# A row DFT moved one pass later, rows normalised four tiles ahead, and nine row tiles transposed by DMA

## The chip, the cores and the metric

The kernel runs on one core of a Trainium2 chip. The metric is the device time of one execution in microseconds (us). A core has a matrix engine (TensorE, PE), a vector engine (VectorE, DVE), an engine for activation functions (ScalarE, ACT), a general one (GpSimd, POOL) and one that does little but issue transfers (SyncE, SP). Each works through its own queue of instructions in order and waits on semaphores for the others; DMA transfers are issued by SP, ACT or POOL and run beside all engines.

## What is computed

The input x has 2048 rows of 576. Its rows are normalised, and two branches work on the result: branch A is a filter in the frequency domain (2D FFT over rows and columns, product with complex weights, inverse), branch B a gated MLP whose gate mixes the 2048 rows with a 2048x2048 matrix.

```python
def _A_ref(x, w_r, w_i):
    X = rfft2(x.astype(float32), axes=(-2, -1))
    X = X * (w_r + 1j * w_i)
    return irfft2(X, s=(S, D), axes=(-2, -1)).astype(bfloat16)

def _B_ref(x, w_in, w_sp, b_sp, w_out):
    z = gelu(einsum('bsd,df->bsf', x, w_in))          # w_in 576 x 4608
    z1 = z[..., :Fh]                                  # Fh = 2304
    z2 = layernorm(z[..., Fh:], axis=-1)
    g = einsum('ts,bsf->btf', w_sp, z2) + b_sp[None, :, None]
    return einsum('bsf,fd->bsd', z1 * g, w_out)

xn = layernorm(A_x, axis=-1)
return A_x + _A_ref(xn, ...) * silu(_B_ref(xn, ...))
```

## The kernel before

**Row tiles and passes.** The 2048 rows are 16 tiles of 128 (m = 0 to 15). For each tile DVE computes mean and variance in `ln1` (L282: two `bn_stats` of 288 columns, L270, and one `bn_aggr`, L274). `rstd_of` (L259) has POOL make the factor 1/sqrt(var + eps) in two small instructions: `ve` (L261) and a power, `pow` (L263). `ln1_apply` (L289) writes the normalised row on DVE into XN, of which there are three buffers (L293, L296). `xpose` (L300) transposes it on TensorE in five blocks of 128x128 (L304), and ACT copies the result from PSUM into xnT (L305). xnT feeds both branches.

**Branch A.** The FFT is a chain of matrix products. `p0_fold` (L309) forms sums and differences of the two halves of a row tile on DVE (L311, L312); FS has four buffers for them. `p0` (L325, with `p0_tail`, L316) is the DFT along the row, on TensorE into PSUM, of which branch A has two buffers. `p0_out` (L332) copies it out on ACT (L334), and **POOL issues the DMA to the scratch Ad in DRAM (L336)**. When all 16 tiles are written, `p1_read` (L342, on SP) reads Ad back the other way round and `p1` (L344) does the first half of the column DFT; p2 (with the weights), p3, p4 and p5 follow, each with a way through DRAM or SBUF between.

**Branch B.** z = gelu(xn @ w_in) comes in chunks. A z2 chunk (L449) is 128 rows by 384 columns; there are 96, six for each row tile. A z1 chunk (L544) is 128 columns by 512 rows; there are 72, and they go to DRAM. Each chunk has four matmuls of 128 rows of contraction and a fifth of 64 (the tail); tails of two chunks at a time are put side by side in the array. z2 rows are normalised like x: for most tiles by six DVE `bn_stats` of chunks (L485), an aggregate (L501), `rstd_of` on POOL and one wide DVE operation (L503). For five tiles ACT makes the sums instead. After the last chunk the mixing with w_sp runs as `main` (L607): a Strassen scheme with seven products P1 to P7 for each of 27 units. It needs sums of z2 blocks (`tsum`, L593, three of a unit) and of slabs of w_sp (`slab_sums`, L536, in parts 0, 1 and 2), both on DVE for the first unit. `outm` (L662) multiplies by w_out and ends the work.

**Order.** Within `tc.manual_schedule` (L740) the instructions of SP, PE and DVE run in the order in which the code issues them; ACT's and POOL's order is chosen by the framework. The chunks fill the time in which branch A waits: `fill(n)` (L709) issues the next n chunks on TensorE in the order of the string `kinds` (L697, "2" for z2, "1" for z1). DVE's work on z2 is queued in `stats_q` and `norm_q`, and `spend` and `z2_stats` (L512, L517) let it out by a running estimate of DVE's and TensorE's load; with `fill(1, 0)` as in the pass loop, hardly any is let out.

**The head and the loop.** The first loads are issued at L247 to L256. From L757 the head normalises tiles 0 to 4 and does passes 0 and 1; the loop of L773 does pass m = 2 to 15. One pass on DVE is fold(m), statistics of tile m+3, apply(m+2); on TensorE it is p0 of the tile, two transposes in every other pass, and two chunks. After the loop come four p1 reads and `fill(11)`.

```python
p0_fold(m)
if m + 3 < MT:
    ln1(m + 3)
if m + 2 < MT:
    ln1_apply(m + 2)
```

Of the kernel before, what the change touches and what calls it, by code (L numbers as in the profile page):

```python
# [90 lines left out]
def kernel(  # L91
# [137 lines left out]

    def load_win_main(t, fs, eng=nc.sync):  # L230
        for a in range(2):
            eng.dma_start(out=t[:, a:KS - 1:2, :], in_=wv[a, 0:2 * P, fs].rearrange("(b p) f -> p b f", p=P))
# [14 lines left out]
    nc.scalar.dma_start(out=ident[:], in_=cd_id.ap())  # L247
    for m0, m1 in ((0, 1), (1, 2), (2, 4)):
        nc.sync.dma_start(out=XC[0][:, m0:m1, :], in_=xv[:, m0:m1, :])
    for n in range(2):  # L250
        load_win_main(WIN2[:, :, n * ZC:(n + 1) * ZC], slice(Fh + n * ZC, Fh + (n + 1) * ZC), nc.scalar)
    for g in range(3):
        (load_win if g else load_win_tail)(WIN2[:, :, 2 * g * ZC:2 * (g + 1) * ZC], slice(Fh + 2 * g * ZC, Fh + 2 * (g + 1) * ZC))
        if g == 0:
            nc.sync.dma_start(out=CDSD, in_=cd_cdsd.ap().rearrange("p (a k l) -> p a k l", a=2, k=3))
        load_x(g + 1)  # L256
    nc.sync.dma_start(out=G1, in_=cd_g1.ap().rearrange("p (s k) -> p s k", s=N2))

    def rstd_of(mv, n, tag):  # L259
        ve = small.tile([P, n], F32, tag=tag + "v")  # L260
        nc.gpsimd.tensor_scalar(out=ve[:], in0=mv[:, :, 1], scalar1=1e-5, scalar2=one[:, 0:1], op0=ALU.add, op1=ALU.mult)  # L261
        rs = small.tile([P, n], F32, tag=tag + "r", bufs=5)
        nc.gpsimd.tensor_tensor(out=rs[:], in0=ve[:], in1=mhalf[:, 0:n], op=ALU.pow)  # L263
        return rs
# [7 lines left out]
    def ln1_aggr(m):  # L272
        mv = small.tile([P, 1, 2], F32, tag="mv1", bufs=5, name="mv1")
        nc.vector.bn_aggr(out=mv[:, 0, :], in_=st1[m][:])  # L274
        if m == 0:
            rs = small.tile([P, 1], F32, tag="l11r", bufs=5, name="rs1")
            nc.scalar.activation(out=rs[:], in_=mv[:, :, 1], func=ACT.Sqrt, bias=eps[:], scale=1.0)
        else:
            rs = rstd_of(mv, 1, "l11")
        ln1_of[m] = (mv[:, 0, 0:1], rs[:, 0:1])  # L280

    def ln1(m):  # L282
        ln1_stats(m)
        ln1_aggr(m)

    st1 = {}
    ln1_of = {}
# [11 lines left out]

    def xpose(m):  # L300
        xn = XN[m % 3]
        pt = psh.tile([P, KS, P], BF16, tag="h")
        for ks in range(KS):
            nc.tensor.transpose(pt[:, ks, :], xn[:, ks * P:(ks + 1) * P], ident[:])  # L304
        nc.scalar.activation(out=xnT[:, m, :, :], in_=pt[:], func=ACT.Identity)  # L305

# [389 lines left out]
    tick = [0]  # L696
    kinds = "2" * 32 + "221" * 11 + "21" * 20 + "221" * 9 + "2111" * 4  # L697
    kinds += "2" * (MT * NZC - kinds.count("2")) + "1" * (FT * 4 - kinds.count("1"))
# [41 lines left out]
    with tc.manual_schedule(engines={SP, PE, DVE}):  # L740
# [19 lines left out]
        ln1_apply(0)  # L760
        nc.scalar.activation(out=THF[:, 0:1], in_=ln1_of[0][1], func=ACT.Gelu_apprx_tanh)
        xpose(0)
        ln1_stats(1, (1,))
        ln1_aggr(1)
        keep_warm(2)
        fill(1, 0)
        ln1(2)
        ln1_apply(1)
        p0_fold(0)
        ln1_apply(2)  # L770
        ln1(3)
        fill(1, 0, lambda: p0_pair(0), lambda: (xpose(1), p0(0, True), xpose(2)))
        p0_fold(1)  # L773
        ln1_apply(3)
        p0(1, False)
        p0_out(1)
        ln1(4)
        fill(1, 0)
        fill(1, 0)
        nc.sync.dma_start(out=MM, in_=cd_mm.ap().rearrange("p (a k) -> p a k", a=3))  # L780
        for m in range(2, MT):
            if m % 2 == 0:
                xpose(m + 1)
            spend(0.78, 2.35 if m + 3 < MT else 0.6)
            p0_fold(m)
            if m + 3 < MT:
                ln1(m + 3)
            if m + 2 < MT:
                ln1_apply(m + 2)
            if m % 2 == 0:  # L790
                fill(1, 0)
                fill(1, 0, lambda: p0_pair(m), lambda: p0(m, True))
            else:
                p0(m, False)
                p0_out(m)
                fill(1, 0)
                if m + 1 < MT:
                    xpose(m + 1)
                fill(1, 0)
            if m in (6, 9):  # L800
                load_win1(m // 9)
        for ch in range(4):
# [17 lines left out]
        for hh in range(0, N2, 2):  # L820
            fill(2)
            if hh + 2 < N2:
                p2(hh + 2)
                spend(0.25, 1.5)
            if hh % 8 != 6:
                fill(1)
            p3(hh)
            spend(0.5)
# [28 lines left out]
        z2_stats(99)  # L857
        for w in (0, 2, 1):
            tsum(0, w)
        later.append(partial(slab_sums, 2, 0, 2))  # L860
# [5 lines left out]
        fill(len(kinds) - place[0])  # L866
        z1_store(None, None)
        assert not stats_q and not norm_q
        for i in range(2):
# [50 lines left out]
```

## Time and profile before

| | |
|---|---|
| median of three runs | 500.8 us (500.46 to 501.24) |
| the profiled execution | 500.46 us, of which the span of the profile is 498.7 us |
| TensorE's clock granted over the span | 1.00 |
| instructions on TensorE | 3454 matmuls in the records (45 row-tile transposes of the change's tiles 7 to 15 among them) |

The slices of the page (40 of 12.5 us each, busy share in tenths) show how the work of the engines lies over the span:

```profile
PE   7999999999999999899999999999999999999996
DVE  5776588798656797965665648856666547877634
ACT  4878777686878656200000011100000011000001
POOL 2665223434242684445535400455454311666600
DMA  7961678978372998672111599021111863111202
```

The first slice holds the loads and the first row tiles, the slices two to four the passes; branch A and the chunks last to about 203 us, and the mixing with w_sp and the product with w_out fill the rest. The costliest groups (columns: line, engine, operation, operands, count, then busy us and mean ns of one, then idle time before and what ended it) that bear on the change:

```profile
L458 PE MATMUL ph<-AR 128*128 128x384 bf16 (+1 forms) x480 | 89.6, 327 | 1.1 <-DMA AR<-in_B_w_in_dram 0.6
L554 PE MATMUL ph<-AR 128*128 128x512 bf16 (+1 forms) x360 | 85.9, 379 | 0.0
L617 PE MATMUL pm<-AR 128*128 128x384 bf16 (+1 forms) x648 | 107.0, 308 | 2.0 <-DVE AR L540 1.9
```

And the transfers that are issued on POOL and read back by SP (columns: KB of one, us from issue to landing):

```profile
Ad<-AR POOLq DMA_DIRECT2D x16, 144.5 KB, 3.6
AR<-Ad SPq DMA_DIRECT2D x4, 578.0 KB, 6.0
```

### The profile page before, as it was taken

The numbers are of one execution on the slowest core, as the hardware profiler recorded it, in microseconds if no ns is written. First come the engines' busy times: TensorE is split into PE (matmuls) and PEld (weight loads), VectorE is DVE, ScalarE is ACT, GpSimd is POOL, SyncE is SP. The second block draws the span as 40 slices with busy tenths as digits, with TensorE's granted clock in tenths as the row PEclk, the third lists the DMA queues.
The fourth block names the chain that finished last, engine by engine and source line by source line (L and its number), as shares of the span: only waits on it lengthen the run. The fifth ranks groups of instructions, "written<-read, shape, count | busy, mean of one in ns | idle before, by whom it ended". The sixth has DMA issues, their size and how long they took to land.

```text
span 498.7 us, 9373 instructions
## 1 busy us (share of the span) xinstructions
PE 488.7 (98%) x3454; PEld 309.5 (62%) x3454; DVE 341.5 (68%) x747; ACT 169.6 (34%) x355; POOL 207.5 (42%) x280
## 2 busy tenths in 40 slices
PE   7999999999999999899999999999999999999996
PEld 3666454555556544466666678666666678888885
DVE  5776588798656797965665648856666547877634
ACT  4878777686878656200000011100000011000001
POOL 2665223434242684445535400455454311666600
PEclk9999999999999999999999999999999999999999
DMA  7961678978372998672111599021111863111202
GB/s 234 312 212 49 251 265 262 315 228 240 109 257 73 242 270 234 202 235 64 33 46 50 125 166 219 27 61 34 48 48 33 174 135 99 50 46 47 76 27 70
DMA packets 86766, 70.67 MB, mean 142 GB/s; under 512 B 39776, under 2 KB 79328, under 8 KB 86464
## 3 DMA queue, kind: packets, MB, share of 16 engines
q1 hardware_dynamic: 80480, 55.54, 41.9%
q0 software_dynamic: 5008, 13.71, 8.2%
q10 hardware_dynamic: 1232, 0.82, 0.5%
q8 instruction: 27, 0.44, 0.4%
q14 instruction: 19, 0.16, 0.1%
HBM read 40.40 MB, written 21.26 MB: 124 GB/s over the span
## 4 chain that ended last, share of the span: by engine, by line
PE 89%; ACT 4%; DVE 3%; DMA 2%; issue 1%; SPq 0%; DVEq 0%; ACTq 0%
PE pm L617 43%; PE po L671 13%; PE ph L554 13%; PE ph L458 12%; PE pb L386 2%; PE pa L329 1%; DMA AR<-in_A_x_dram 1%; PE pa L428 1%; PE pa L374 1%; ACT AR L334 1%; ACT Z_74 L471 1%; PE pa L350 1%; ACT Z_74 L477 1%; PE pa L402 1%; DMA AR<-c_cdsd 1%
## 5 line engine op out<-in xcount | busy, mean ns | idle before, releaser
L617 PE MATMUL pm<-AR,Z_74 128*128 128x384 bf16 (+1 forms) x864 | 138.7, 308 | 0.0
L621 DVE TENSOR_TENSOR AR<-pm,AR 128x384 f32<-128x384 f32 (+3 forms) x162 | 82.4, 513 | 70.2 <-PE pm L617 66.5
L617 PEld LDWEIGHTS <-Z_74 128*128 128x128 bf16 x864 | 84.5, 98 | 40.6
L617 PE MATMUL pm<-AR 128*128 128x384 bf16 (+1 forms) x648 | 107.0, 308 | 2.0 <-DVE AR L540 1.9
L458 PE MATMUL ph<-AR 128*128 128x384 bf16 (+1 forms) x480 | 89.6, 327 | 1.1 <-DMA AR<-in_B_w_in_dram 0.6
L554 PE MATMUL ph<-AR 128*128 128x512 bf16 (+1 forms) x360 | 85.9, 379 | 0.0
L617 PEld LDWEIGHTS <-AR 128*128 128x128 bf16 x648 | 63.3, 98 | 32.8 <-DVE AR L540 2.2
L631 ACT ACTIVATE AR<-pm 128x384 f32<-128x384 f32 (+1 forms) x27 | 12.3, 455 | 187.4 <-PE pm L617 187.4
L671 PE MATMUL po<-AR 128*128 128x288 bf16 x540 | 66.6, 286 | 0.0
L671 PEld LDWEIGHTS <-AR 128*128 128x128 bf16 x594 | 56.9, 98 | 13.9
L458 PEld LDWEIGHTS <-AR 128*128 128x128 bf16 (+1 forms) x480 | 40.0, 97 | 36.8 <-issue 14.5
L605 POOL TENSOR_TENSOR AR<-Z_74,AR 128x1024 bf16<-128x1024 bf16 x26 | 55.3, 2128 | 12.1 <-PE pm L617 12.1
L632 POOL TENSOR_TENSOR AR<-AR 128x384 f32<-128x384 f32 (+1 forms) x27 | 22.9, 849 | 79.7 <-ACT AR L631 75.6
L574 POOL DMA_DIRECT2D Z1d<-AR x55 | 32.0, 582 | 55.7 <-ACT AR L563 53.2
L554 PEld LDWEIGHTS <-AR 128*128 128x128 bf16 (+1 forms) x360 | 30.2, 97 | 28.1 <-issue 5.5
L563 ACT ACTIVATE AR<-ph 128x512 bf16<-128x512 f32 x72 | 42.1, 593 | 15.6 <-PE ph L554 15.4
L477 ACT ACTIVATE Z_74<-ph 128x384 bf16<-128x384 f32 x66 | 31.9, 500 | 23.4 <-PE ph L458 23.2
L674 ACT ACTIVATE TH<-po 128x576 f32<-128x576 f32 x15 | 9.8, 651 | 77.8 <-PE po L671 77.8
L635 POOL TENSOR_TENSOR AR<-AR 128x384 f32<-128x384 f32 (+1 forms) x27 | 30.1, 1114 | 12.5 <-DVE AR L621 12.5
L628 DVE TENSOR_TENSOR AR<-AR 128x384 bf16<-128x384 bf16 (+1 forms) x108 | 31.7, 334 | 0.9
L680 DVE SCALAR_TENSOR_TENSOR AR<-TH,po 128x576 bf16<-128x576 f32 x15 | 11.3, 754 | 30.0 <-ACT TH L674 29.9
L686 POOL DMA_DIRECT2D out_dram<-AR x12 | 6.6, 548 | 52.4 <-DVE AR L684 46.0
(186 smaller groups left out, 504.0 us busy)
## 6 DMA issues: line engine op xcount, KB each, us to landing
Z1d<-AR POOLq DMA_DIRECT2D x55, 128.0 KB, 4.2
AR<-Z1d SPq DMA_DIRECT2D x36, 192.0 KB, 3.0
AR<-in_A_x_dram SPq DMA_DIRECT2D x18, 144.0 KB, 2.7
AR<-in_B_w_out_dram SPq DMA_DIRECT2D x1, 2592.0 KB, 10.9
Ad<-AR POOLq DMA_DIRECT2D x16, 144.5 KB, 3.6
AR<-Ad SPq DMA_DIRECT2D x4, 578.0 KB, 6.0
AR<-in_A_w_r_dram SPq DMA_DIRECT2D x16, 144.5 KB, 3.5
AR<-in_A_w_i_dram SPq DMA_DIRECT2D x16, 144.5 KB, 4.1
```

Of the source, the lines that this page charges most:

```text
L458: nc.tensor.matmul(self.ph[:], lhsT=xnT[rows, self.m, ks, :], rhs=WIN2[rows, ks, n * ZC:(n + 1) * ZC], start=start, stop=stop)
L477: nc.scalar.activation(out=zc, in_=ph[:], func=ACT.Gelu_apprx_tanh)
L554: nc.tensor.matmul(self.ph[:].rearrange("p (a t) -> p a t", a=4), lhsT=wb[rows, ks, (fi % WG) * P:(fi % WG + 1) * P], rhs=xnT[rows, 4 * tq ...
L563: nc.scalar.activation(out=zs, in_=ph[:], func=ACT.Gelu_apprx_tanh)
L574: (nc.sync if place[0] > len(kinds) - 16 else nc.gpsimd).dma_start(out=d, in_=s_)
L605: (nc.gpsimd if u else nc.vector).tensor_tensor(out=t, in0=zblk(p, 1, 0), in1=t2, op=ALU.subtract)
L617: nc.tensor.matmul(dst, lhsT=z[:, s, :], rhs=SLB[SA[name]][:, s, 0:nt], start=(s == 0 and not more), stop=(s == HM - 1), skip_group_check= ...
L621: nc.vector.tensor_tensor(out=out, in0=x, in1=y, op=ALU.add)
L628: nc.vector.tensor_tensor(out=o, in0=o, in1=zb[:, f, h, 0:nt], op=ALU.mult)
L632: nc.gpsimd.tensor_tensor(out=p1b, in0=p1, in1=B[1], op=ALU.add)
L635: nc.gpsimd.tensor_tensor(out=ux, in0=p1a, in1=B[0], op=ALU.add)
L671: nc.tensor.matmul(pv[:, hh, :], lhsT=U[:, fi, h, i * P:(i + 1) * P], rhs=WOUT[:, fi, c0 + hh * H2:c0 + hh * H2 + w // nh], start=(fi == 0 ...
```

## The change

1. First loads. ACT issues only ident and one half (a = 0) of the first z2 chunk's weights; the other half, and both halves of the second chunk's, go by SP between the single row tiles x0, x1, x2 and x3. Both groups of z1 weights (WIN1) are loaded in the head instead of after passes 6 and 9. G1 comes in two halves after passes 9 and 11, MM after the loop. ACT executes one Sqrt early.
2. Normalisation of the first tiles. Tile 1 too takes ACT's Sqrt and DVE's reciprocal; `ve` of tiles 2 and 3 runs on DVE; xnT of tile 0 is copied by DVE.
3. Passes. The loop begins at m = 0. A pass on DVE is fold(m), apply(m+4), statistics of tile m+5, so that a row is applied four tiles ahead of its fold. 36 chunks lie before the end of the passes (before 32), and `kinds` is changed to match.
4. Tiles 7 to 15 are transposed by a DMA transpose from XN to xnT, issued on SP straight after their apply; tiles 0 to 6 as before.
5. Later fills: `p3` of the last columns has no fill after hh = 24, and so the chunks shift to later places.
6. Two of the first unit's three `tsum` come after the last fill instead of before the last fills.

On POOL, whose order the framework chooses, these are the instructions of the passes after the change, in order (`DMA` is the Ad write of one tile, L336): ve, pow of tile 4; of 5; ve 6, DMA 0, pow 6; DMA 1; 7; 8; DMA 2; 9; DMA 3; 10; DMA 4, 5, 6; 11; DMA 7; 12; 13; ve 14, DMA 8, pow 14; DMA 9; 15; DMA 10 to 13; ve, pow of z2 tile 0; DMA 14, 15; then the writes of z1.

```diff
--- before.py
+++ after.py
@@ -227,8 +227,8 @@
     HT = H2 - 2 * P
     wv = B_w_in.rearrange("(a d) f -> a d f", a=2)
 
-    def load_win_main(t, fs, eng=nc.sync):
-        for a in range(2):
+    def load_win_main(t, fs, eng=nc.sync, halves=(0, 1)):
+        for a in halves:
             eng.dma_start(out=t[:, a:KS - 1:2, :], in_=wv[a, 0:2 * P, fs].rearrange("(b p) f -> p b f", p=P))
 
     def load_win_tail(t, fs):
@@ -245,20 +245,30 @@
         load_win(wb, fs)
 
     nc.scalar.dma_start(out=ident[:], in_=cd_id.ap())
-    for m0, m1 in ((0, 1), (1, 2), (2, 4)):
-        nc.sync.dma_start(out=XC[0][:, m0:m1, :], in_=xv[:, m0:m1, :])
-    for n in range(2):
-        load_win_main(WIN2[:, :, n * ZC:(n + 1) * ZC], slice(Fh + n * ZC, Fh + (n + 1) * ZC), nc.scalar)
+    wh = [(WIN2[:, :, n * ZC:(n + 1) * ZC], slice(Fh + n * ZC, Fh + (n + 1) * ZC)) for n in range(2)]
+
+    def load_row(m):
+        nc.sync.dma_start(out=XC[0][:, m, :], in_=xv[:, m, :])
+
+    load_row(0)
+    load_win_main(*wh[0], nc.scalar, (0,))
+    nc.scalar.activation(out=THF[:, 1:2], in_=eps[:], func=ACT.Sqrt)
+    load_win_main(*wh[0], nc.sync, (1,))
+    load_row(1)
+    load_win_main(*wh[1], nc.sync)
+    load_row(2)
     for g in range(3):
         (load_win if g else load_win_tail)(WIN2[:, :, 2 * g * ZC:2 * (g + 1) * ZC], slice(Fh + 2 * g * ZC, Fh + 2 * (g + 1) * ZC))
         if g == 0:
+            load_row(3)
             nc.sync.dma_start(out=CDSD, in_=cd_cdsd.ap().rearrange("p (a k l) -> p a k l", a=2, k=3))
         load_x(g + 1)
-    nc.sync.dma_start(out=G1, in_=cd_g1.ap().rearrange("p (s k) -> p s k", s=N2))
-
-    def rstd_of(mv, n, tag):
+    for g in range(2):
+        load_win1(g)
+
+    def rstd_of(mv, n, tag, eng=nc.gpsimd):
         ve = small.tile([P, n], F32, tag=tag + "v")
-        nc.gpsimd.tensor_scalar(out=ve[:], in0=mv[:, :, 1], scalar1=1e-5, scalar2=one[:, 0:1], op0=ALU.add, op1=ALU.mult)
+        eng.tensor_scalar(out=ve[:], in0=mv[:, :, 1], scalar1=1e-5, scalar2=one[:, 0:1], op0=ALU.add, op1=ALU.mult)
         rs = small.tile([P, n], F32, tag=tag + "r", bufs=5)
         nc.gpsimd.tensor_tensor(out=rs[:], in0=ve[:], in1=mhalf[:, 0:n], op=ALU.pow)
         return rs
@@ -272,17 +282,18 @@
     def ln1_aggr(m):
         mv = small.tile([P, 1, 2], F32, tag="mv1", bufs=5, name="mv1")
         nc.vector.bn_aggr(out=mv[:, 0, :], in_=st1[m][:])
-        if m == 0:
+        if m < 2:
             rs = small.tile([P, 1], F32, tag="l11r", bufs=5, name="rs1")
             nc.scalar.activation(out=rs[:], in_=mv[:, :, 1], func=ACT.Sqrt, bias=eps[:], scale=1.0)
         else:
-            rs = rstd_of(mv, 1, "l11")
+            rs = rstd_of(mv, 1, "l11", nc.vector if m < 4 else nc.gpsimd)
         ln1_of[m] = (mv[:, 0, 0:1], rs[:, 0:1])
 
     def ln1(m):
         ln1_stats(m)
         ln1_aggr(m)
 
+    DT = 7
     st1 = {}
     ln1_of = {}
 
@@ -297,12 +308,18 @@
                                 in0=xr[:, None, :, 2 * P:H2].to_broadcast((P, 2, 2, HT)), scalar1=mean, scalar2=rs,
                                 op0=ALU.subtract, op1=ALU.mult)
 
-    def xpose(m):
+    def xpose_dma(m):
+        nc.sync.dma_start_transpose(out=xnT[:, m, :, :], in_=XN[m % 3].rearrange("p (k i) -> p k i", k=KS))
+
+    def xpose(m, eng=nc.scalar):
         xn = XN[m % 3]
         pt = psh.tile([P, KS, P], BF16, tag="h")
         for ks in range(KS):
             nc.tensor.transpose(pt[:, ks, :], xn[:, ks * P:(ks + 1) * P], ident[:])
-        nc.scalar.activation(out=xnT[:, m, :, :], in_=pt[:], func=ACT.Identity)
+        if eng is nc.scalar:
+            nc.scalar.activation(out=xnT[:, m, :, :], in_=pt[:], func=ACT.Identity)
+        else:
+            eng.tensor_copy(out=xnT[:, m, :, :], in_=pt[:])
 
     Adw = Ad[:].rearrange("(c m p) l -> m p c l", c=2, p=P)
 
@@ -694,7 +711,7 @@
     zq = iter(range(MT * NZC))
     yq = iter(range(FT * 4))
     tick = [0]
-    kinds = "2" * 32 + "221" * 11 + "21" * 20 + "221" * 9 + "2111" * 4
+    kinds = "2" * 36 + "221" * 10 + "21" * 20 + "221" * 8 + "2111" * 4
     kinds += "2" * (MT * NZC - kinds.count("2")) + "1" * (FT * 4 - kinds.count("1"))
     held = []
     place = [0]
@@ -758,35 +775,35 @@
         ln1_stats(1, (0,))
         nc.vector.reciprocal(out=ln1_of[0][1], in_=ln1_of[0][1])
         ln1_apply(0)
-        nc.scalar.activation(out=THF[:, 0:1], in_=ln1_of[0][1], func=ACT.Gelu_apprx_tanh)
-        xpose(0)
         ln1_stats(1, (1,))
         ln1_aggr(1)
+        nc.scalar.activation(out=THF[:, 0:1], in_=ln1_of[1][1], func=ACT.Gelu_apprx_tanh)
+        xpose(0, nc.vector)
+        nc.vector.reciprocal(out=ln1_of[1][1], in_=ln1_of[1][1])
+        ln1_apply(1)
         keep_warm(2)
         fill(1, 0)
+        xpose(1)
         ln1(2)
-        ln1_apply(1)
-        p0_fold(0)
+        fill(1, 0)
+        ln1(3)
         ln1_apply(2)
-        ln1(3)
-        fill(1, 0, lambda: p0_pair(0), lambda: (xpose(1), p0(0, True), xpose(2)))
-        p0_fold(1)
-        ln1_apply(3)
-        p0(1, False)
-        p0_out(1)
         ln1(4)
         fill(1, 0)
+        ln1_apply(3)
+        xpose(2)
         fill(1, 0)
-        nc.sync.dma_start(out=MM, in_=cd_mm.ap().rearrange("p (a k) -> p a k", a=3))
-        for m in range(2, MT):
-            if m % 2 == 0:
-                xpose(m + 1)
-            spend(0.78, 2.35 if m + 3 < MT else 0.6)
+        for m in range(MT):
+            if m % 2 == 0 and m + 3 < DT:
+                xpose(m + 3)
+            spend(0.9 if m + 3 < DT else 0.6, 0.5 + 0.6 * (m + 4 < MT) + 1.0 * (m + 5 < MT))
             p0_fold(m)
-            if m + 3 < MT:
-                ln1(m + 3)
-            if m + 2 < MT:
-                ln1_apply(m + 2)
+            if m + 4 < MT:
+                ln1_apply(m + 4)
+                if m + 4 >= DT:
+                    xpose_dma(m + 4)
+            if m + 5 < MT:
+                ln1(m + 5)
             if m % 2 == 0:
                 fill(1, 0)
                 fill(1, 0, lambda: p0_pair(m), lambda: p0(m, True))
@@ -794,11 +811,13 @@
                 p0(m, False)
                 p0_out(m)
                 fill(1, 0)
-                if m + 1 < MT:
-                    xpose(m + 1)
+                if m + 3 < DT:
+                    xpose(m + 3)
                 fill(1, 0)
-            if m in (6, 9):
-                load_win1(m // 9)
+            if m in (9, 11):
+                hf = slice((m - 9) * N2 // 4, (m - 7) * N2 // 4)
+                nc.sync.dma_start(out=G1[:, hf, :], in_=cd_g1.ap().rearrange("p (s k) -> p s k", s=N2)[:, hf, :])
+        nc.sync.dma_start(out=MM, in_=cd_mm.ap().rearrange("p (a k) -> p a k", a=3))
         for ch in range(4):
             p1_read(ch)
         load_w(0)
@@ -822,7 +841,7 @@
             if hh + 2 < N2:
                 p2(hh + 2)
                 spend(0.25, 1.5)
-            if hh % 8 != 6:
+            if hh % 8 != 6 and hh < 26:
                 fill(1)
             p3(hh)
             spend(0.5)
@@ -855,8 +874,7 @@
         load_z1(0)
         tick[0] += 4
         z2_stats(99)
-        for w in (0, 2, 1):
-            tsum(0, w)
+        tsum(0, 0)
         later.append(partial(slab_sums, 2, 0, 2))
         assert place[0] > kinds.rindex("2")
         nc.sync.dma_start(out=BB, in_=B_b_sp.rearrange("(a s) -> a s", a=1).to_broadcast((P, S)))
@@ -865,6 +883,8 @@
             slab_sums(i, 0, 1)
         fill(len(kinds) - place[0])
         z1_store(None, None)
+        for w in (1, 2):
+            tsum(0, w)
         assert not stats_q and not norm_q
         for i in range(2):
             slab_sums(i, 0, 2)
```

## The prediction

> **What bounds the kernel now.** I read the busy shares first, then the chain that ended last, then windows of ten microseconds (per engine: busy us and instructions, in the order PE, weight load, DVE, ACT, POOL, SP; then granted clock, DMA share, GB/s):
>
> ```profile
> PE 488.7 (98%) x3454; PEld 309.5 (62%) x3454; DVE 341.5 (68%) x747; ACT 169.6 (34%) x355; POOL 207.5 (42%) x280
> PE 89%; ACT 4%; DVE 3%; DMA 2%; issue 1%; SPq 0%; DVEq 0%; ACTq 0%
> 30.00:40.00 10.00, 9.85 (x87) 6.09 (x84) 7.59 (x28) 8.27 (x17) 6.79 (x13) 1.00 0.37 106
> 200.00:210.00 10.00, 8.15 (x48) 4.03 (x47) 9.90 (x16) 2.77 (x5) 3.87 (x6) 1.00 0.65 193
> ```
>
> TensorE bounds it, at full clock. An edit helps if it takes TensorE instructions away or closes one of its few gaps; it hurts if it opens a gap. There are about 10 us of gaps to win: half in the first 13 us, 1.9 us at 206, the rest in pieces. So I looked at the places where a TensorE instruction waits, and at the chain of row normalisation that the change re-orders. In the timeline (start, duration, engine, line, [idle before, releaser]), first the cycle of one row tile on DVE and POOL:
>
> ```profile
> 10.98 0.81 DVE L270 BATCH_NORM_STATS2 st_180<-AR 128x6 f32<-128x288 bf16 x2
> 11.82 0.21 DVE L274 BATCH_NORM_AGGREGATE mv_183<-st_180 128x2 f32<-128x12 f32 x1
> 12.21 0.32 POOL L261 TENSOR_SCALAR ve<-mv_183,one 128x1 f32<-128x1 f32 x1 [2.25 <-DVE AR L311]
> 12.60 0.55 POOL L263 TENSOR_TENSOR rs<-ve,mhalf 128x1 f32<-128x1 f32 x1
> 13.19 0.41 DVE L293 TENSOR_SCALAR AR<-AR,mv_183,rs 128x512 bf16<-128x512 bf16 x1 [0.80 <-POOL rs L263]
> 13.74 0.82 DVE L270 BATCH_NORM_STATS2 st_238<-AR 128x6 f32<-128x288 bf16 x2
> ...
> 40.60 0.29 DVE L311 TENSOR_TENSOR AR<-AR 128x256 bf16<-128x256 bf16 x1 [1.28 <-ACT AR L305]
> 43.44 0.41 DVE L293 TENSOR_SCALAR AR<-AR,mv_712,rs 128x512 bf16<-128x512 bf16 x1 [0.46 <-POOL rs L263]
> 45.55 0.29 DVE L311 TENSOR_TENSOR AR<-AR 128x256 bf16<-128x256 bf16 x1 [1.47 <-ACT AR L305]
> ```
>
> The reader is to see that from aggregate to apply of the same tile POOL needs 1.37 us (11.82 to 13.19), with 0.80 us of DVE idle although a fold lay between. In the other passes another tile's statistics lie there, the idle time is before the fold, and its releaser is TensorE's transpose with ACT's copy. A pair of passes takes 4.95 us (40.60 to 45.55).
>
> Then the way from the last row tile to the column DFT:
>
> ```profile
> 46.73 0.28 DVE L312 TENSOR_TENSOR AR<-AR 128x256 bf16<-128x256 bf16 x1
> 55.35 0.32 DVE L501 BATCH_NORM_AGGREGATE mv<-st_847 128x2 f32<-128x36 f32 x1
> ...
> 49.35 1.56 POOL L336 DMA_DIRECT2D Ad<-AR  x2 [3.67 <-ACT AR L334]
> 55.77 0.26 POOL L261 TENSOR_SCALAR ve<-mv,one 128x1 f32<-128x1 f32 x1 [1.77 <-DVE mv L501]
> 56.12 0.57 POOL L263 TENSOR_TENSOR rs<-ve,mhalf 128x1 f32<-128x1 f32 x1
> ...
> 53.53 2.23 SPq L342 DMA_DIRECT2D AR<-Ad  x4
> ...
> 48.27 3.19 PE L458 MATMUL ph<-AR 128*128 128x384 bf16 x19
> 59.13 0.41 PE L350 MATMUL pa<-AR 128*128 128x289 bf16 x2
> ```
>
> The last Ad writes leave POOL at 49.35, six microseconds before POOL's first z2 statistics (55.77). TensorE covers 48.27 to 59.13 with fills, and the column DFT starts without a gap.
>
> **What the Trainium skill says.** "Advanced Engine Details and Errata", X-Bar Transpose (TRN2), calls transpose DMAs as fast as regular ones, 350-400 GB/s. The source view of L534 shows 256 KB ones issuing in 1.31 us (median) and landing in 4.4. "SBUF — State Buffer", Who interferes with whom, says that a DVE operation with two SBUF inputs contends with GpSimd reads. It agrees with the trace as far as it goes: `pow` takes 0.55 us alone and up to 0.83 beside folds. "TensorE: Matmul & The Clock Gate", Why this matters for your kernels, warns of idle gaps over about 3 us; the trace of before has none so long and shows no drop.
>
> **Part by part.**
> *Transposes.* 45 TensorE transposes go. Five of them advance TensorE by 0.28 us (33.90 to 34.18 in its timeline), so 9 tiles x 0.28 = -2.5 us of TensorE work, but only where TensorE is the bound. ACT loses nine copies of 0.75 us (L305), which nobody on the path waits for afterwards. TensorE's demand for a pair is then four chunk bodies x 0.65, tails 0.33 and 0.25, two p0 x 0.50 = 4.18 us, against 4.74 with transposes.
>
> *Pass order on DVE.* Each pass becomes fold(m), apply(m+4), stats and aggregate(m+5). Apply(m+4) follows the aggregate of its own tile with only a fold between: the cycle of 10.98 to 13.74, 2.76 us a pass, 5.52 a pair. TensorE needs 4.2 to 4.7 and before ran at 4.95. Being one pass ahead gives DVE no room, since it is DVE's own chain that is slower; what was saved on TensorE turns into waits for folds. Twelve such cycles (tiles 4 to 15) from 11.3, then four passes at 2.1: the 36 chunks that now belong to the passes end at 53.2. In before 32 are done at 49.4, and four more x 0.74 make 52.4. That is +0.8 us.
>
> *POOL's queue.* The Ad writes are issued on POOL, 0.73 us each (L336), waiting for ACT's copy of p0. In the new POOL order the write of tile 0 stands ahead of tile 6's `pow`, the writes of tiles 4 to 6 ahead of tile 11's, that of tile 8 ahead of tile 14's. A write waiting for p0 now holds the chain: +0.75, about +1.4 (tile 6's p0 ends late in the pass), +0.75 = +2.9, of which the bounds are 0 and 3.5. With the head about -0.2: stage +3.5, between 0 and +4.5.
>
> *Head.* ident, one quarter of W and x0 go first, x1 later behind W. x1 lands at about 4.8 instead of 3.92 (an estimate from the queue's rate), x2 and x3 no longer together. DVE takes the xnT(0) copy and the `ve` of tiles 2 and 3. My recurrence puts the first useful TensorE work 0.9 us earlier; X1 is behind fewer tails. Bounds -0.9 and +1.5, because DMA is full from 2 to 7 us; I take it as part of the -0.2 above. WIN1's twelve DMAs move from passes 6 and 9 to the head: SP's queue is free of them by about 27 us, tile 7's transpose is due at about 19. G1 and MM later have 17 us to spare: no cost for either.
>
> *Crossbar transposes.* SP issues nine of 160 KB; by size I estimate 0.9-1.3 us of issue and 3.5-4 of landing from the 256 KB ones. Fold(k) is four passes after apply(k), over 10 us; XN's reuse three passes later, over 8 us. Cost 0. If one blocked SP for over 2.76 us it would set the pass (a rival).
>
> *Start of p1.* The z2 statistics of tile 0 (18 bn_stats, then aggregate) follow fold(15) at once on DVE, and their `ve`/`pow` stand on POOL **ahead of the Ad writes of tiles 14 and 15**. Before, that pair of POOL instructions came after the writes. Fold(15) end to POOL free is 56.69 - 47.01 = 9.7 us; then two writes issue, the second at +0.75; it lands in 3.2; the read issue 0.14; it lands in 4.4 (the minimum of L342). Sum 18.2 us after fold(15). TensorE covers p0(15) end to p1 with 10.86 us of fills (59.13 - 48.27). Fold(15) runs ahead of p0(15) by X: it waits for apply(15) plus the transpose's landing, about 5.5 us after fold(11), while TensorE takes four passes, 8.4 + 1, so X is about 3.6, 2.5 to 4. Gap = 18.2 - 10.86 - X = 7.3 - X = +3.75 to +4.85: I take +4, with 0 for X over 7.3 and up to +1.7 more if the idle gap costs the clock.
>
> *End of the fills.* At 200 to 210 DVE is full (9.90 of 10) and the second product waits 1.85 us for L540. Two tsums of 0.62 us now come after L540's first sums, so it starts 1.24 us earlier, and the next product waits a little for its own tsum: -1.0, between -1.4 and 0. Fills taken from p3 and given to the fills after it: TensorE work is the same and the profile shows no gap there; 0, bounds ±0.5.
>
> **Sum.** +3.5 +4.0 -1.0 = +6.5 on the profiled execution's span of 498.7, whose time is 500.46; the three runs' median is 500.8. So 507.3, I say 507.
>
> **Rivals.**
> A, as above, 0.60: 503 to 511.
> B, faster, 0.15: POOL's answer is covered after all. If a cycle takes at most 2.1 us (TensorE's demand), passes stay with TensorE: 8 pairs x about 0.4 and the head's 0.9 make about -4, DVE runs far enough ahead that X passes 7.3, so no gap at p1, and tsum gives -1.0: about 495.5. It breaks even at about 2.5 us a cycle. For it: DVE idles 1.3 us a pair in before. Against: the 0.80 us wait with a fold in place.
> C, one of the two costs only, 0.18: chain without POOL's writes (+0.8) with the gap (+4) -1, or the chain (+3.5) without the gap -1: 503 to 505.
> D, 0.07: a transpose out of SBUF takes longer on SP's queue than a pass, say 5 us: 9 x (5 - 2.76) = +20, about 521.
>
> **How the numbers follow.** A and C together lie in 502 to 511; the bounds of head and clock widen that. D and most of B are left out: 501 to 512. This kernel's runs can tell 0.2%, 1 us, from no change. Faster 0.14 (B, nearly), same 0.04 (the edges of B and C), slower 0.82.
>
> **What would show it.** Right: L311 or L293 waits on POOL rs of 0.5 us and more in most passes; TensorE idle before L329 from 15 to 45 us; an Ad write issued after a `pow` of z2 near 60 us and TensorE idle 3 to 5 us before L350 there; the wait of the second product at 206 shrunk. Wrong: passes of 4.2 us a pair with DVE waiting for TensorE or for DMA; L350 without a gap; transposes on SP that take 3 us or more.

## The result, and the profile after

The changed kernel takes 513.35 us (median of four runs, 513.13 to 514.61) against 501.02 of the kernel before in the same comparison: a ratio of 1.0252, with a 95% interval of 1.0231 to 1.0272. It is slower by 12.3 us where 6.5 were forecast. The profiled execution took 513.56 us with a span of 511.8, 13.1 more than the span before.

First the busy shares and the chain that ended last of the changed kernel, then a window in the passes and one at the start of p1 (same columns as before):

```profile
PE 490.5 (96%) x3409; PEld 308.1 (60%) x3409; DVE 342.4 (67%) x751; ACT 164.0 (32%) x347; POOL 206.0 (40%) x276
PE 84%; DVE 5%; DMA 4%; POOL 2%; issue 2%; ACT 2%; SPq 0%; DVEq 0%; ACTq 0%; POOLq 0%
...
30.00:40.00 10.00, 8.08 (x59) 4.29 (x56) 6.30 (x23) 5.13 (x11) 6.24 (x11) 1.00 0.56 132
70.00:80.00 10.00, 7.46 (x39) 3.84 (x39) 4.17 (x8) 4.19 (x8) 1.59 (x4) 0.83 0.95 338
```

TensorE has 45 instructions less and yet more busy time, since part of it ran at a lower clock (0.83 in the second window); in the chain, POOL has come in and the shares of DVE and DMA have grown. In the passes no engine is full any more (TensorE 8.08 of 10, before 9.85): work is waiting, not running. At four places the loss can be read off:

| | before | after | |
|---|---|---|---|
| last p0 of tile 15 ends | 48.27 | 56.86 | +8.6, of which 4 chunks x 0.74 are work done earlier: +5.6 |
| first product of p1 starts | 59.13 | 72.53 | +4.8 more |
| first product of the mixing starts | 202.77 | 215.24 | the 4 chunks come back: +2.0 more |
| end of the span | 498.7 | 511.8 | +0.6 |

The DVE and POOL timelines of the changed kernel in the passes:

```profile
12.63 0.31 DVE L307 TENSOR_SCALAR AR<-AR,mv_189,rs 128x128 bf16<-128x128 bf16 x1
13.11 0.82 DVE L280 BATCH_NORM_STATS2 st_219<-AR 128x6 f32<-128x288 bf16 x2 [0.17 <-DMA AR<-in_A_x_dram]
...
19.48 0.21 DVE L284 BATCH_NORM_AGGREGATE mv_304<-st_301 128x2 f32<-128x12 f32 x1
21.67 0.41 DVE L304 TENSOR_SCALAR AR<-AR,mv_304,rs 128x512 bf16<-128x512 bf16 x1 [1.63 <-POOL rs L273]
24.45 0.41 DVE L304 TENSOR_SCALAR AR<-AR,mv_347,rs 128x512 bf16<-128x512 bf16 x1 [0.81 <-POOL rs L273]
...
46.34 0.81 DVE L280 BATCH_NORM_STATS2 st_648<-AR 128x6 f32<-128x288 bf16 x2
```

```profile
19.79 0.39 POOL L271 TENSOR_SCALAR ve<-mv_304,one 128x1 f32<-128x1 f32 x1 [1.74 <-DVE mv_304 L284]
20.12 0.93 POOL L353 DMA_DIRECT2D Ad<-AR  x1
21.07 0.56 POOL L273 TENSOR_TENSOR rs<-ve,mhalf 128x1 f32<-128x1 f32 x1
```

Every apply from tile 5 on waits on POOL: 0.80 to 0.82 us for most tiles, 1.63 for tile 6, whose `ve` and `pow` have an Ad write between them (20.12), 1.97 for tile 11 and 1.60 for tile 14, for which Ad writes stand in the way likewise. From the statistics of tile 4 (13.11) to those of tile 15 (46.34) are eleven passes in 33.2 us: 11 x 2.76 = 30.4, and 2.9 for the writes on POOL. TensorE waits for the folds:

```profile
23.49 0.67 PE L346 MATMUL pa<-AR 128*128 128x290 bf16 x4 [1.12 <-DVE AR L328]
29.03 0.67 PE L346 MATMUL pa<-AR 128*128 128x290 bf16 x4 [0.81 <-DVE AR L328]
34.58 0.67 PE L346 MATMUL pa<-AR 128*128 128x290 bf16 x4 [1.11 <-DVE AR L328]
41.28 1.15 PE L346 MATMUL pa<-AR 128*128 128x290 bf16 x4 [1.43 <-DVE AR L328]
```

From the last fold to p1, in the timelines of DVE, POOL and TensorE:

```profile
54.29 0.29 DVE L328 TENSOR_TENSOR AR<-AR 128x256 bf16<-128x256 bf16 x1 [3.23 <-DMA AR<-AR]
54.50 0.28 DVE L329 TENSOR_TENSOR AR<-AR 128x256 bf16<-128x256 bf16 x1
63.11 0.32 DVE L518 BATCH_NORM_AGGREGATE mv<-st_823 128x2 f32<-128x36 f32 x1
...
63.54 0.26 POOL L271 TENSOR_SCALAR ve<-mv,one 128x1 f32<-128x1 f32 x1 [8.54 <-DVE mv L518]
63.88 0.56 POOL L273 TENSOR_TENSOR rs<-ve,mhalf 128x1 f32<-128x1 f32 x1
64.40 1.48 POOL L353 DMA_DIRECT2D Ad<-AR  x2
...
67.06 0.82 PE L475 MATMUL ph<-AR 128*128 128x384 bf16 x4
72.53 0.64 PE L367 MATMUL pa<-AR 128*128 128x289 bf16 x2 [4.65 <-DMA AR<-Ad]
72.97 1.91 PE L571 MATMUL ph<-AR 128*128 128x512 bf16 x4
```

The two last Ad writes leave POOL only at 64.40, behind the first z2 statistics, and TensorE stands still for 4.65 us. What follows takes 1.91 us instead of about 1.03: half the clock.

### The profile page after: what moved, and what is told of

Read it like the earlier page. It is cut to its first block, busy times and chain, and to the rows that moved or that the text cites. A ratio compares the mean times of both kernels' runs of the same rounds, so it can differ in the third digit from the quotient of the medians.

```text
span 511.8 us, 9300 instructions
## 1 busy us (share of the span) xinstructions
PE 490.5 (96%) x3409; PEld 308.1 (60%) x3409; DVE 342.4 (67%) x751; ACT 164.0 (32%) x347; POOL 206.0 (40%) x276
## 4 chain that ended last, share of the span: by engine, by line
PE 84%; DVE 5%; DMA 4%; POOL 2%; issue 2%; ACT 2%; SPq 0%; DVEq 0%; ACTq 0%; POOLq 0%
PE pm L634 41%; PE po L688 13%; PE ph L571 12%; PE ph L475 10%; PE pb L403 2%; DMA AR<-in_A_x_dram 1%; POOL rs L273 1%; PE pa L445 1%; PE pa L367 1%; PE pa L391 1%; DMA AR<-in_B_w_in_dram 1%; PE pa L346 1%; DMA AR<-Ad 1%; PE pa L419 1%; DVE AR L304 1%
## 5 line engine op out<-in xcount | busy, mean ns | idle before, releaser
L648 ACT ACTIVATE AR<-pm 128x384 f32<-128x384 f32 (+1 forms) x27 | 12.3, 455 | 188.2 <-PE pm L634 188.2
L475 PEld LDWEIGHTS <-AR 128*128 128x128 bf16 (+1 forms) x480 | 40.7, 98 | 39.3 <-issue 18.1
L622 POOL TENSOR_TENSOR AR<-Z_74,AR 128x1024 bf16<-128x1024 bf16 x26 | 55.2, 2124 | 12.1 <-PE pm L634 11.3
L571 PEld LDWEIGHTS <-AR 128*128 128x128 bf16 (+1 forms) x360 | 30.7, 98 | 28.5 <-issue 4.6
L697 DVE SCALAR_TENSOR_TENSOR AR<-TH,po 128x576 bf16<-128x576 f32 x15 | 11.3, 754 | 30.0 <-ACT TH L691 29.9
L393 DVE TENSOR_TENSOR AR<-pa,AR 128x578 bf16<-128x578 f32 x32 | 22.8, 752 | 8.5 <-PE pa L391 7.4
## 6 DMA issues: line engine op xcount, KB each, us to landing
AR<-in_B_w_out_dram SPq DMA_DIRECT2D x1, 2592.0 KB, 11.3
Ad<-AR POOLq DMA_DIRECT2D x16, 144.5 KB, 3.8
AR<-in_A_w_r_dram SPq DMA_DIRECT2D x16, 144.5 KB, 3.7
```

What stands on the lines that cost most here:

```text
L393: nc.vector.tensor_tensor(out=tt[:, c, :, :], in0=pa[:, :, 0:L], in1=wt[:, c, hh % 4:hh % 4 + 2, :], op=ALU.mult)
L475: nc.tensor.matmul(self.ph[:], lhsT=xnT[rows, self.m, ks, :], rhs=WIN2[rows, ks, n * ZC:(n + 1) * ZC], start=start, stop=stop)
L571: nc.tensor.matmul(self.ph[:].rearrange("p (a t) -> p a t", a=4), lhsT=wb[rows, ks, (fi % WG) * P:(fi % WG + 1) * P], rhs=xnT[rows, 4 * tq ...
L622: (nc.gpsimd if u else nc.vector).tensor_tensor(out=t, in0=zblk(p, 1, 0), in1=t2, op=ALU.subtract)
```

## The experiments

Theory 1 is that of the prediction: two waits, the one in the passes (aggregate, POOL, apply) and the one of the Ad writes behind z2's statistics, are the loss. The rivals put it on the DMA transposes, on the order of the loads, or on the later chunk order. All runs are of the whole kernel. They were made in four comparisons, in which the kernel before had medians of 499.97 to 500.17 us; in the comparison with the changed kernel it had 501.02. So differences of a microsecond between runs of different comparisons are read against the kernel before of each.

### The two waits, one at a time and together

```diff
+            if m + 5 < MT:
+                ln1(m + 5)
             if m + 4 < MT:
                 ln1_apply(m + 4)
...
-            if m + 5 < MT:
-                ln1(m + 5)
```

> The changed kernel with one exchange in the pass loop: statistics of tile m+5 before the apply of tile m+4. Theory 1 (the chain aggregate - POOL - apply sets the pass): statistics cover POOL's answer, passes fall back to TensorE's demand, two pairs of 4.74 and five of 4.18 us = 30.4 from the second p0 to the last, instead of 39.0 (17.37 to 56.35); no slow clock at 41 us; the gap before p1 stays or shrinks. 513.3 - 8.6 = 504.7, 500 to 506. Rival (the DMA transposes or the full DMA queues hold the folds): passes stay at 5.5 us a pair and the time at 512 to 514.

507.48 us, above the expected 500 to 506. From the second p0 (17.62) to the last (49.92) are 32.3 us, against 39.0: the wait in the passes is the loss that theory 1 says, though 30.4 were expected, since TensorE's pair without transposes takes 4.37 us and not 4.18, and the first three pairs took 4.66 to 5.21. The gap before p1 grew by 1.0 us:

```profile
67.07 0.64 PE L367 MATMUL pa<-AR 128*128 128x289 bf16 x2 [5.62 <-DMA AR<-Ad]
```

TensorE now comes earlier to p1, while POOL still writes tiles 14 and 15 behind the z2 statistics (at 57.93).

```diff
-        nc.gpsimd.dma_start(out=Adw[m], in_=sg[:, :, 0:L])
+        (nc.scalar if m >= 14 else nc.gpsimd).dma_start(out=Adw[m], in_=sg[:, :, 0:L])
```

> The changed kernel, with the Ad writes of tiles 14 and 15 issued by ACT behind its own copy instead of by POOL. Theory 1 (these two writes stand behind the first z2 statistics on POOL): the last write is issued near 58.5 instead of 65.2 us, p1's data lands near 66.6 and the fills last until 67.9: no gap, -4.8, and no slow clock behind it, -1.3: 507.2 us. Rival (p1 waits for the read itself, or for G1 and MM that are loaded late): the gap stays at 3 us or more, 511 to 514 us.

506.69 us, beside the 507.2 of theory 1. ACT's queue and TensorE in the timeline:

```profile
57.56 0.37 ACTq L353 DMA_DIRECT2D Ad<-AR  x1
58.88 0.37 ACTq L353 DMA_DIRECT2D Ad<-AR  x1
...
67.17 0.82 PE L475 MATMUL ph<-AR 128*128 128x384 bf16 x4
67.83 0.41 PE L367 MATMUL pa<-AR 128*128 128x289 bf16 x2
68.08 1.02 PE L571 MATMUL ph<-AR 128*128 128x512 bf16 x4
68.94 0.41 PE L367 MATMUL pa<-AR 128*128 128x289 bf16 x2
69.19 0.81 PE L475 MATMUL ph<-AR 128*128 128x384 bf16 x4
```

No gap, and from the first p1 product to the z2 chunk after the second (67.83 to 69.19) 1.36 us, where the changed kernel needs 2.63: the slow clock behind the gap cost 1.27.

> Both edits together: statistics of tile m+5 before the apply of tile m+4, and the Ad writes of tiles 14 and 15 on ACT. If the two costs are independent and are the whole of the loss, 513.3 - 8.6 - 6.1 = 498.6 us, some 2 us under the kernel before. If the gap had already gone with the first edit, the sum is smaller: 500 to 505. If a third cost exists (the later chunk order, the transposes by DMA), it stays above 503 us.

499.52 us (498.67 to 502.47), ratio to the kernel before 0.9997 (0.9981 to 1.0013). Against the kernel before of the same comparison, the changed kernel loses 12.3 us, stats_first 7.5, ad_on_act 6.7, and both_orders nothing (its median is 0.5 lower, within the interval). So one edit alone brings 4.8, the other 5.6, both together 12.8 us: the two waits and what hangs on them are the whole loss. The two alone add up to less, partly because the gap and the slow clock behind it grew in stats_first. What else the change brings, good and bad, comes to about nothing; beside the trace of the kernel before, and with the four chunks allowed for that lie in the passes now, the passes of both_orders end 1.3 us earlier, from p1 to the mixing it takes 0.7 us more, and from the mixing to the end 0.7 less.

### The two parts of the wait in the passes

```diff
-        nc.gpsimd.dma_start(out=Adw[m], in_=sg[:, :, 0:L])
+        nc.scalar.dma_start(out=Adw[m], in_=sg[:, :, 0:L])
```

> The changed kernel with all sixteen Ad writes issued by ACT, so that POOL holds nothing but ve and pow in the passes; the order of apply and statistics stays that of the change. The prediction's two terms for the passes are told apart: DVE's waits on POOL for tiles 6, 11 and 14 (1.63, 1.97, 1.60 us in the changed kernel) fall to the 0.80 of all others, 2.8 us less than ad_on_act (506.7): 503.9 us, and the pure cycle of 2.76 us a pass remains. Rival (the writes cost nothing, the chain alone is the loss): 506.7 us.

507.74 us, not 503.9. The waits on POOL are what was expected, 0.80 us for every tile, 6, 11 and 14 too. But another wait came in, of an apply for the DMA transpose that reads the XN buffer which it is to overwrite:

```profile
35.44 0.41 DVE L304 TENSOR_SCALAR AR<-AR,mv,rs 128x512 bf16<-128x512 bf16 x1 [3.49 <-DMA AR<-AR]
```

and SP's own queue (waited for: us, times, longest) shows why:

```profile
SPq L232 <- DMA Ad<-AR: 4.6, 2, 4.3
```

SP's loads of the z1 weights waited 4.3 us for an Ad write which ACT had issued, and the first DMA transpose, queued behind them, went out at 31.64 instead of 26.72. TensorE waited 2.00 us at 35.35 and 1.48 at 37.25. So POOL's share is confirmed by the waits, but its 2.8 us aren't confirmed by the time; the rival's 506.7 lies nearer.

### The tsums

The first run puts the three tsums back in the changed kernel; the second moves the two in the kernel before and changes nothing else.

> The changed kernel, with the three tsums of the first unit back at the place that they have in the kernel before. The prediction had the move at -1.0: then this run is 1.0 us slower than the changed kernel. The trace of the changed kernel shows the second product waiting 1.50 us and the fourth 0.81: with the tsums back the fourth's wait goes and the second's grows by the two tsums, 1.2: +0.4 us. Rival: the move costs by itself, -0.5 us.

515.06 us, 513.81 to 516.19: slower, but the profiled execution shows where it lost time, and it isn't there: TensorE waited 2.20 us at 7.2 for its first transpose, and in the five us after that the clock was 0.53 and 0.50. Tile 4's statistics start 1.67 us later than in the changed kernel (14.78), and the last p0 comes 1.73 us later (58.08). At the end the second product waits 1.85 us and no later one does, so that the fifth starts 7.23 us after the first, as in the kernel before. In ad_on_act, with the tsums moved, it is 6.16; in the profiled execution of the changed kernel 7.84, where ACT had been held 0.87 us by a write of z1 to DRAM (Z1d; the copies of p5 came late, and with them all of DVE). Its time doesn't decide. The traces tell more: from the first product of the mixing to the end of the span are 295.9 us in the kernel before and in tsum_back, 294.7 to 295.3 in the fourteen other profiled executions with the move, and 296.6 only in that of the changed kernel.

> The kernel before with the move of the two tsums alone. The prediction: the second product starts 1.24 us earlier, the fourth waits a little, -1.0 us: 499.0 beside 500.0 of the kernel before. Rival (the fourth product gives it back, as the trace of the changed kernel shows): within 0.3 us of the kernel before.

499.01 us (498.75 to 499.39), ratio 0.9975 (0.9966 to 0.9985): the move brings 1.16 us. TensorE's timeline of it:

```profile
202.76 1.46 PE L617 MATMUL pm<-AR,Z 128*128 128x384 bf16 x8
204.75 1.48 PE L617 MATMUL pm<-AR 128*128 128x384 bf16 x8 [0.53 <-ACT AR L631]
206.06 1.47 PE L617 MATMUL pm<-AR,Z 128*128 128x384 bf16 x8
```

The second product's wait falls from 1.85 to 0.53 us, and it no longer ends with the slab sum but with ACT's copy.

### DMA transposes and the order of the loads

All of these start from both_orders, in which the DVE chain no longer covers anything.

```diff
-    DT = 7
+    DT = 16
```

> both_orders with all 16 tiles transposed on TensorE (no DMA transposes). If the prediction's price holds, 45 transposes bring back 9 x 0.28 = 2.5 us of TensorE work, less the 0.35 us that the first DMA transpose delays a fold: 501.7 us. Rival (DMA transposes cost what they save, by waits of DVE and by traffic): at or below 499.5 us.

501.23 us (500.89 to 502.32): the DMA transposes bring 1.7 us of the 2.5 of TensorE's work, or 1.5 if each run is set against the kernel before of its own comparison. Without them the runs lie closer together than those of both_orders.

```diff
+    for m0, m1 in ((0, 1), (1, 2), (2, 4)):
+        nc.sync.dma_start(out=XC[0][:, m0:m1, :], in_=xv[:, m0:m1, :])
+    for n in range(2):
+        load_win_main(*wh[n], nc.scalar)
     nc.scalar.activation(out=THF[:, 1:2], in_=eps[:], func=ACT.Sqrt)
-    load_win_main(*wh[0], nc.sync, (1,))
-    load_row(1)
-    load_win_main(*wh[1], nc.sync)
...
```

> no_crossbar with the first loads in the order of the kernel before. Without DMA transposes the load order is tested by itself: p0 starts at 15.1 instead of 16.2 us, 501.2 - 1.1 = 500.1 us. Rival (other loads are then late): 501 us or more.

500.08 us: the load order of the kernel before is worth 1.15 us. In the traces the statistics of tile 4 start at 12.23 instead of 13.25. The same in both_orders, with the DMA transposes:

> both_orders, with the first loads in the order of the kernel before (x0, x1, x2 and x3 together on SP; four parts of the z2 weights on ACT). Theory (the new order delays x1 behind the weights, from 3.9 to 5.3 us, and leaves TensorE waiting up to 2 us at its first transposes, at times with a slow clock behind it): 1.0 us less and a narrower spread than the 498.7 to 502.5 of both_orders: 498.5 us. Rival (the head is bound by the weights or by the DVE chain): no difference, 499.5 us with the same spread.

501.00 us, 497.55 to 503.97: p0 starts 1.2 us earlier (15.07), the spread is wider and the median worse. In the profiled execution the last transposes land late and a fold waits:

```profile
DMA to landing us min/median/max: 3.1/4.4/9.6
...
48.87 0.29 DVE L325 TENSOR_TENSOR AR<-AR 128x256 bf16<-128x256 bf16 x1 [7.78 <-DMA AR<-AR]
```

> both_orders with the z1 weights loaded after passes 6 and 9 as before. In both_orders the first DMA transpose is issued behind these twelve loads on SP near 27 us and DVE waits 2.98 us at 31 us for it; here the wait goes, and with it TensorE's 0.35 us: 499.1 us. Rival: the loads fall between transposes instead and delay those (1 us of SP for two, 2 us for four): 499.5 to 501 us.

503.08 us, beyond the rival too. The first transpose does go out earlier (22.63), but the twelve loads now stand between the later ones; that of tile 14 lands after 7.9 us, and TensorE waits for its fold (the profiled execution, 501.52 us, is the fastest of the four):

```profile
50.20 0.29 DVE L325 TENSOR_TENSOR AR<-AR 128x256 bf16<-128x256 bf16 x1 [7.48 <-DMA AR<-AR]
...
44.82 2.76 PE L472 MATMUL ph<-AR 128*128 128x384 bf16 x16
50.55 0.67 PE L343 MATMUL pa<-AR 128*128 128x290 bf16 x4 [2.97 <-DVE AR L325]
```

> old_loads with G1 in one piece in the head, as in the kernel before, instead of two halves among the last transposes. Theory (a DMA transpose that shares the queue with G1 and the Ad writes lands after 5 to 9.6 instead of 2.6 us, and folds 14 and 15 wait): landings of at most 5 us, no fold waits over 0.5 us, 498.5 us with a spread under 2 us. Rival (Ad writes alone slow the transposes, or G1 in the head delays X2 and X3): 500 to 502 us with the wide spread of old_loads.

504.19 us, and beyond the rival again. The landings are at most 5.0 us now, but with G1 in front of it the first transpose goes out at 28.47, and TensorE waits 3.30 us for it at 33.55. So in passes at TensorE's own rate, each of these three orders of SP's queue makes some transpose late, at its issue or at its landing, while in both_orders TensorE waited only once for a fold in the passes, 0.35 us. Which order would keep all of them in time wasn't found.

### The chunk order, and the head

> no_crossbar with the chunk order string of the kernel before. The wait of 1.10 us at the fourth p4 product, which stands in every run of the changed chunk order, comes from ACT's accumulations meeting ACT's p4 copy there; with the old string it falls to the 0.45 of the kernel before: -0.65, 500.6 us beside 501.2. Rival: the wait stays at 1.1, no difference.

501.31 us, no difference; p4's fourth product still waits for ACT's copy, 1.17 us in the timeline against 0.93 in no_crossbar and 0.15 in the kernel before. The string isn't the cause.

```diff
-        fill(12)
+        fill(10)
         for u in range(4 * NLC):
```

> no_crossbar_old_loads with fill(10) instead of fill(12) ahead of p4, so that p4 meets the same place in the chunk order as in the kernel before (the change puts it two chunks later). Theory (ACT's accumulations of a z2 tile meet ACT's p4 copy by that shift): the wait of 1.10 us falls to 0.45: 499.4 us beside 500.1. Rival (the wait has another cause, or two chunks fewer let p4 wait for its reads): 500.1 or more.

499.46 us, 0.62 less (0.44 if each run is set against the kernel before of its own comparison); in the traces it is 0.8 less from p1 to the mixing. The wait has shrunk to 0.18:

```profile
148.54 0.61 PE L416 MATMUL pa<-AR 128*128 128x128 bf16 x8
149.33 0.61 PE L416 MATMUL pa<-AR 128*128 128x128 bf16 x8 [0.18 <-ACT AR L423]
```

Four chunks more in the passes and two fewer in p3 put p4 two chunks later. There ACT makes the sums of a z2 tile just before p4's copy (161.05 to 163.07 in the changed kernel's timeline).

The last term is the head. In the changed kernel DVE waits for ACT's gelu table (ACT's and DVE's timelines), because the activation behind the load reads the factor that DVE's reciprocal overwrites:

```profile
7.51 1.28 ACT L780 ACT_TABLE_LOAD   x1
8.81 0.20 ACT L780 ACTIVATE TH<-rs_158 128x1 f32<-128x1 f32 x1
...
9.04 0.16 DVE L782 RECIPROCAL rs_158<-rs_158 128x1 f32<-128x1 f32 x1 [1.41 <-ACT TH L780]
```

```diff
-        nc.scalar.activation(out=THF[:, 0:1], in_=ln1_of[1][1], func=ACT.Gelu_apprx_tanh)
         xpose(0, nc.vector)
         nc.vector.reciprocal(out=ln1_of[1][1], in_=ln1_of[1][1])
+        nc.scalar.activation(out=THF[:, 0:1], in_=ln1_of[1][1], func=ACT.Gelu_apprx_tanh)
```

> no_crossbar_old_loads, with the reciprocal of tile 1 on DVE ahead of ACT's gelu table load instead of behind it (the load reads the factor that the reciprocal overwrites, and DVE waits 1.52 us for it). Theory: apply(1) and transpose(1) come 1.5 us earlier, TensorE's wait of 1.47 us at 7.5 shrinks; part is given back, since x of tiles 4 to 7 lands at 11.6: -1.0, 499.1 us beside 500.1. Rival (the landing of x sets the head whatever DVE does): -0.2 or nothing.

499.90 us, nothing beyond the noise (499.24 to 503.16). The wait for the table is gone, and in the profiled execution DVE waits for x of tiles 4 to 7 in its place, as the rival says:

```profile
12.64 0.82 DVE L277 BATCH_NORM_STATS2 st<-AR 128x6 f32<-128x288 bf16 x2 [1.98 <-DMA AR<-in_A_x_dram]
```

That load landed 12.6 us into the execution, 1.0 later than in no_crossbar_old_loads, so what the edit is worth when it lands early stays open.

> Both edits of head_no_war and p4_place: 500.1 - 1.0 - 0.65 = 498.4 us, under the kernel before by 1.7 and under before_tsum by 0.6. If only one works: 499.1 to 499.5.

498.86 us in the median, 0.6 less than p4_place, but 498.40 to 503.00, ratio 0.9992 (0.9976 to 1.0009): not surely better than the kernel before. Surely better are p4_place by 0.5 us, ratio 0.9989 (0.9982 to 0.9995), and before_tsum, 499.01 us, by 1.2.

## Why the prediction was wrong

The direction and both mechanisms were right, and all four signs that the prediction named came; the size was half. The sum of the prediction, term by term, on the profiled executions:

| term | predicted | measured | from |
|---|---|---|---|
| cycle of 2.76 us a pass, writes on POOL +2.9 | +3.7 | +3.8 | the passes' +5.6 less the head; 33.2 us for eleven cycles: 30.4 + 2.9 |
| head | -0.2 | +1.8 | statistics of tile 4 at 13.11, not 11.3 |
| gap before p1 | +4.0 | +4.65 | wait of L367 |
| slow clock behind the gap | 0, up to 1.7 | +1.27 | 2.63 against 1.36 us |
| p4 | 0 | +0.4 to +0.8 | p4_place |
| tsum | -1.0 | -1.16 alone; +0.6 in the profiled execution | before_tsum; 7.84 against 7.23 us |

With the profiled execution's values that is some 12.8 of the 13.1 us of span; 0.3 us aren't assigned.

**The step that failed most is the head.** The prediction put it at -0.2 and let the chain start at 11.3, which is 2.4 us earlier than the kernel before does it (13.74). It started at 13.11, and two things held it there, each by itself. DVE was busy almost without a pause from 9.04 to 12.94: x1 had landed at 5.35 and not at 4.8, and then DVE waited 1.41 us for ACT's table load, for which the prediction has no term. And the second load of x, which tile 4 needs, landed at 13.1: its issue had moved from 7.89 to 6.82, but it took 6.3 us instead of 5.3. In passes bound by that chain, each us of late start is a us of the end, as tsum_back shows (1.67 later at the start, 1.73 at the last p0). The bound of the head (+1.5) was too narrow, and taking its middle hid it. no_crossbar_old_loads shows the part that the load order has in it, 1.0 us at tile 4's statistics, though in passes that the chain doesn't bind; head_no_war shows that without the table load's wait DVE can meet the wait for x instead.

**The clock was put at nothing** although the step named it and priced it. In all three traces with the gap open, TensorE came out of it slowly: from the first product of p1 to that of the mixing are 142.7 us here, 143.4 in stats_first and 143.5 in tsum_back, against 141.4 in ad_on_act and both_orders. The sum should have held it.

**The gap** came near by luck, since two errors met. X, the lead of fold(15) over p0(15), was 56.86 - 54.78 = 2.1 and not 3.6, outside its stated 2.5 to 4: tile 15's transpose took 4.9 us to land (beside Ad writes and half of G1), not 3.5 to 4, and the fold waited 3.23 us for it. By the prediction's 7.3 - X that makes 5.2. But from fold(15) to p1's data were 17.75 us and not 18.2, and the fills covered 11.0 and not 10.86: 17.75 - 11.0 - 2.1 = 4.65. That fold, with 0.57 us before fold(14), is where the DMA transposes, priced at 0, cost time in the changed kernel.

**tsum** was right by itself. That the changed kernel lost 0.6 at that place is read from one trace alone (ACT held by a Z1d write) and stands in no other; whether its other executions lost it isn't known.

**p4** was priced at 0 with bounds of 0.5, and took about 0.6.

**Slips in the sums.** Twelve cycles of 2.76 us and four passes of 2.1 from 11.3 end at 52.8 and not at 53.2, so the chain's own +0.8 is +0.4; and 7.3 - X with X from 2.5 to 4 gives a gap of 3.3 to 4.8. Neither decides the outcome.

Of the rivals, B was far off: a cycle takes 2.76 us and not 2.1. D didn't happen: no transpose held SP for 2.76 us (1.35 at most in the changed kernel, 2.36 in late_win1). But late_win1 and old_loads_g1_head show something near it: once the chain is mended, a transpose that is late in SP's queue or at its landing holds TensorE (2.97 and 3.30 us).

## What to carry to other kernels

When an edit puts a consumer straight behind the producer of its operand on the same in-order engine, the round trip over the second engine (here 1.37 us over POOL) becomes part of every pass, whatever is "ahead" by several tiles; put independent work between them. In the order of a queue that nobody wrote by hand, look for the last writes of a stage: one that stands behind the first instruction of the next stage moves the whole stage (here a gap of 4.65 us, and 1.3 of slow clock behind it). And transfers that are free beside a slow chain are not free beside a fast one: price them again once the chain is mended.

## What the runs showed of the hardware

A slow clock needn't cost anything. In the changed kernel TensorE also ran slowly from 41.28: four p0 products took 1.15 us instead of 0.67, and the granted clock from 42 to 44 us was 0.50, after several idle stretches of at most 1.43 us and none of 3. In ad_on_act's profiled execution the clock there was full after idle stretches as long, and p0 of tile 15 ended at 56.76 instead of 56.86, since the fold would have been waited for anyway. In all_ad_on_act waits of 2.00 and 1.48 us were followed by sixteen chunk products in 4.70 us instead of 2.76. Here the Trainium skill ("TensorE: Matmul & The Clock Gate", Why this matters for your kernels), which warns of gaps over about 3 us, and the traces differ, and the traces decide: the clock fell without such a gap. What decides it isn't shown here, as the same waits came with and without it.

A DMA transpose of 160 KB from SBUF took SP 1.20 to 1.35 us to issue in the changed kernel. The nine landed there in 2.6 to 4.9 us (median 2.8), the Ad writes of 144.5 KB in 2.7 to 5.8 (3.8). In old_loads both were slower, 3.1 to 9.6 us (4.4) and 2.5 to 8.9 (5.4). "Advanced Engine Details and Errata", X-Bar Transpose (TRN2), which calls transposes as fast as regular transfers, agrees with both; what the prediction missed is how late either kind can land among others. No run here shows the bandwidth that the page gives.

ACT's table load took 1.28 us, as the Trainium skill has it ("ScalarE: Activation LUTs", What ACT_TABLE_LOAD costs, about 1283 ns). The page adds a drain and comes to about 2.66 us for a switch; here, from the end of the activation before the load to the start of the one after it, were 1.32 us (7.49 to 8.81), and the trace decides.
